# A windowed attention feeding a GELU MLP on one core: new order of the early attention stage, and of each batch's first transposes

## The chip, the cores and the metric

One Trainium2 chip, and on it one core. The metric is device time in microseconds of one execution, median of several runs. Inputs and output are fp32 in HBM; the kernel computes in fp16 with fp32 sums.

## What is computed

```python
def _attn_ref(q, k, v):                    # each 8 x 8 x 576 x 64 (batch, head, position, dim)
    scores = scale * np.matmul(q, k.transpose(0, 1, 3, 2))
    mask = np.abs(pos[:, None] - pos[None, :]) <= 32
    scores = np.where(mask, scores, -1000000000.0)
    attn = np.exp(scores - np.max(scores, axis=-1, keepdims=True))
    attn = attn / (np.sum(attn, axis=-1, keepdims=True) + 1e-09)
    return np.matmul(attn, v)

def _moe_ref(x, w_in, w_out):              # x 4608 x 512, w_in 512 x 2048, w_out 2048 x 512
    h = x @ w_in
    c = np.float32(np.sqrt(2.0 / np.pi))
    g = 0.5 * h * (1.0 + np.tanh(c * (h + 0.044715 * h * h * h)))
    return g @ w_out
```

Every position sees its 32 neighbours on each side. The eight heads' outputs, side by side, are the 512 features of a token, and all 8 x 576 = 4608 tokens go through the two-layer MLP.

## The kernel before

**Attention by pairs and units.** A batch has four pairs of heads (`pr`), and a pair has two units (`u = 2*pr` and `u = 2*pr + 1`), each for one half of the positions. The steps of a pair and a unit, by function and line of the kernel before:

- `cast_pair` (L199) casts a pair's q and k from fp32 to fp16; `trans_pair` (L209) transposes them on TensorE in eight matmuls against the identity `idn` (L213, L215) into the one PSUM tile `pt` of the pool `psT`, and DVE copies them out into `QT` (L216) and `KT` (L217). `cast_tail` (L182) and `trans_tail` (L188, four matmuls at L192, copies at L194 and L197) do the same for the last 64 positions of all pairs of a batch, in the same PSUM tile.
- `scores` (L243): six matmuls (L251) into `ps_s`, one tile of two banks; ACT's Exp (L258) out of it to `pe`; DVE's multiply with the band mask to `pm` (L260). The next `scores` needs `ps_s` empty.
- `values` (L265): twelve matmuls (L278) into `ps_od`, one tile of two banks, half of them against V, half against ones, which gives the denominators; ACT's Ln (L285) and Exp with scale -1 (L287) make their reciprocals `rt`; DVE multiplies into `xT` (L296), a ring of 2048 tokens. The next `values` needs `ps_od` empty, that is, this multiply done.

**The MLP by tiles of 512 tokens.** `ffn_in(t, fc)` (L302) is one group of four matmuls of 512 columns (L309) into a bank `ph` of the pool `psM` (three banks, tag `mm`), followed by ACT's GELU (L313). Sixteen such groups are the first product of a tile t. `ffn_out(t, i)` (L318) is one matmul of 512 columns (L323) into `py` (also `psM`); each sixteenth ends with DVE's copy `yo` (L327) and the store. Sixty-four of them are the second product of a tile.

**Order of the work.** Each engine runs its instructions in the order in which the program writes them. The program has three stages.

1. Early attention of batches 0 and 1 (L340 to L358): per pair POOL's casts of q, k and V, the transposes, (with pair 0) the tail, and then `scores` of each unit with `values` of the unit before.
2. The first product of tiles 0 and 1 together, over four quarters of `w_in` (L361 to L368); then the casts of `w_out` and the loads of batch 2 (L369 to L372). SP's loads wait for buffers that the casts release (`stage`, three buffers).
3. For t = 0 to 8 (L375 on): the first product of the tile (from t = 2), then its 64 matmuls of the second. For t = 0 to 5 batch b = t + 2 is computed among those 64. `put(i, ...)` fixes ahead of which matmul i a step stands, by `TRANS` (0, 13, 25, 37 for the pairs' transposes; the tail two later, the next pair's cast four later), `FIRST`, `STEP` and `LAG` (scores of unit u at 8 + 6u, values at 18 + 6u). Each such t starts with a load of ACT's Exp table, the loads of batch b + 1, `cast_tail(b)` and `cast_pair(b, 0)` on DVE.

Of the kernel before, what the change touches and what calls it, by code (L numbers as in the profile page):

```python
# [26 lines left out]
SW = 416  # L27

FIRST, STEP, LAG = 8, 6, 10
TRANS = (0, 13, 25, 37)


RING = 2048
# [3 lines left out]
def kernel(  # L39
# [96 lines left out]
    def load_w_in(i):  # L136
        w = stage.tile([128, 4, 512], FP32, name="wst", tag="stage", padded_shape=[128, 5, 512])
        nc.sync.dma_start(w, w_in_v[:, :, 512 * i:512 * i + 512])
        return w
# [122 lines left out]
            op=ALU.mult)  # L262
        units[(b, u)] = pm

    def values(b, u):  # L265
        pr, hf = u // 2, u % 2
        pm = units.pop((b, u))
        V = Vs[b % 2]
        od = psO.tile([128, 2, 512], FP32, name="ps_od")
        off = 0  # L270
        last = len(PIECES[hf]) - 1
        for i, (c, p0, p1) in enumerate(PIECES[hf]):
            n = p1 - p0
            a, e = p0 - HALF * hf, p1 - HALF * hf
            for w in range(2):
                for h in range(2):
                    r0 = 64 * h
                    nc.tensor.matmul(  # L278
                        od[r0:r0 + 64, w, 0:4 * HALF].rearrange("d (j p) -> d j p", j=4)[:, :, a:e],
                        V[:, c, 2 * pr + h, :] if w == 0 else ones,  # L280
                        pm[:, h, off:off + 4 * n].rearrange("k (j p) -> k j p", j=4),
                        start=(i == 0), stop=(i == last), skip_group_check=True)
            off += 4 * n
        lt = ap_.tile([128, 4 * HALF], FP32, name="lt")
        nc.scalar.activation(lt, od[:, 1, 0:4 * HALF], AF.Ln)  # L285
        rt = ap_.tile([128, 4 * HALF], FP32, name="rt")
        nc.scalar.activation(rt, lt, AF.Exp, scale=-1.0)  # L287
        o3 = od[:, 0, 0:4 * HALF].rearrange("d (j p) -> d j p", j=4)
# [29 lines left out]
    def ffn_out(t, i):  # L318
# [6 lines left out]
        if fc == NF - 1:  # L325
# [5 lines left out]
            while g < end:  # L331
# [4 lines left out]
                m += e - g  # L336
                g = e


    for b in range(2):  # L340
        cast_tail(b)
        V, vr = Vs[b], raws[b][3]
        for pr in range(NPAIR):
            cast_pair(b, pr, nc.gpsimd)
            nc.gpsimd.tensor_copy(V[:, 0:4, 2 * pr:2 * pr + 2, :], vr[:, 0:4, 2 * pr:2 * pr + 2, :])
            nc.gpsimd.tensor_copy(V[0:64, 4, 2 * pr:2 * pr + 2, :], vr[0:64, 4, 2 * pr:2 * pr + 2, :])
            trans_pair(b, pr)
            if pr == 0:
                trans_tail(b)
            for u in (2 * pr, 2 * pr + 1):  # L350
                scores(b, u)
                if u > 0:
                    values(b, u - 1)
                elif b:
                    values(b - 1, 7)
    wi = [load_w_in(0)]
    cast_w(wi[0], w_in16[:, :, 0:512])
    values(1, 7)  # L358


    for g in range(4):  # L361
        if g < 3:
            wi.append(load_w_in(g + 1))
        for t in range(2):
            for fc in range(4 * g, 4 * g + 4):
                ffn_in(t, fc)
                if t == 0 and fc == 4 * g + 1 and g < 3:
                    cast_w(wi[g + 1], w_in16[:, :, 512 * g + 512:512 * g + 1024])  # L368
    for g in range(4):  # L369
        cast_w(load_w_out(g), w_out16[:, 4 * g:4 * g + 4, :])  # L370
    load_qk(2, False)
    load_v(2)  # L372


    for t in range(NT):  # L375
        if t >= 2:
            for fc in range(NF):
                ffn_in(t, fc)
        b = t + 2
        at = {}  # L380

        def put(i, fn, *args):
            at.setdefault(i, []).append((fn, args))

        if b < B:
            load_exp_table()
            if b + 1 < B:
                load_qk(b + 1, False)
                load_v(b + 1)
            cast_tail(b)  # L390
            cast_pair(b, 0)
            for pr in range(NPAIR):
                put(TRANS[pr], trans_pair, b, pr)
                if pr == 0:
                    put(TRANS[pr] + 2, trans_tail, b)
                if pr < 3:
                    put(TRANS[pr] + 4, cast_pair, b, pr + 1)
            for u in range(8):
                put(FIRST + STEP * u, scores, b, u)
                put(FIRST + STEP * u + LAG, values, b, u)  # L400
        for i in range(64):
            for fn, args in at.pop(i, []):
                fn(*args)
            ffn_out(t, i)
        assert not at
# [28 lines left out]
```

## Time and profile before

| | |
|---|---|
| median of 3 runs | 385.72 us (385.48 to 386.09) |
| the profiled execution | 384.81 us, span 383.1 us, granted TensorE clock 0.994 |
| busy, share of the span | PE 90%, PEld 45%, ACT 55%, DVE 41%, POOL 15% |
| chain that ended last, by engine | PE 81%, DVE 8%, ACT 7%, issue 2%, POOL 1% |
| moved by DMA | 43.02 MB, mean 112 GB/s |

PE is the matmuls of TensorE, PEld its weight loads, which run beside them; DVE is VectorE, ACT ScalarE, POOL GpSimd, SP the engine that issues most loads and all stores. The profiled execution is one run; its time holds the span from the first to the last instruction and 1.7 us around it. The busy shares are of the whole span. The chain is followed back from the last instruction, at each step to what released it. A granted clock of 1.00 stands for 2.4 GHz, the higher of two levels; the lower is 1.2 GHz.

### The profile page before, as it was taken

Reading aid. Unit: us, or ns where it says so; the run is one execution under the profiler, and the core shown is the slowest. Engines: PE = TensorE matmul, PEld = TensorE weight load, DVE = VectorE, ACT = ScalarE, POOL = GpSimd, SP = SyncE. Lnnn points to the kernel's source line nnn. Section 1 sums busy time; section 2 is a strip of 40 time slices with the busy share of each in tenths; the row PEclk is TensorE's granted clock in tenths of the full one; section 3 lists DMA queues with packets and bytes.
Section 4 is the critical chain, followed back from the end, with each engine's and each line's share of the span. In section 5 each row is a group of like instructions: output and inputs, shape, how many; then the busy total and the mean of one; then the engine's idle time right before and its main releaser. Section 6 shows DMA issues by size and latency. Waiting matters only on the chain.

```text
span 383.1 us, 6525 instructions
## 1 busy us (share of the span) xinstructions
PE 343.9 (90%) x2592; PEld 171.8 (45%) x2592; DVE 158.0 (41%) x379; ACT 209.6 (55%) x349; POOL 59.4 (15%) x97
## 2 busy tenths in 40 slices
PE   2656559999979999999999999999999999999995
PEld 1445444444534444454445444444444444444442
DVE  3546544415755860585058504850485002011011
ACT  1545466665662676567656765767566721611610
POOL 8542501581040040004000400000000000000000
PEclk9999999999998999999999999999999999999999
DMA  7988307999779269117911692100011012003012
GB/s 198 267 219 276 112 3 242 384 286 215 95 69 285 68 68 280 19 55 68 272 27 44 74 264 41 56 29 27 2 55 29 27 30 78 6 27 82 2 33 77
DMA packets 72894, 43.02 MB, mean 112 GB/s; under 512 B 47776, under 2 KB 64160, under 8 KB 72864
## 3 DMA queue, kind: packets, MB, share of 16 engines
q1 hardware_dynamic: 44736, 39.07, 34.9%
q0 software_dynamic: 28128, 3.54, 14.5%
q8 instruction: 20, 0.33, 0.3%
q14 instruction: 10, 0.08, 0.1%
HBM read 36.70 MB, written 9.44 MB: 120 GB/s over the span
## 4 chain that ended last, share of the span: by engine, by line
PE 81%; DVE 8%; ACT 7%; issue 2%; POOL 1%; DVEq 0%
PE ph L309 33%; PE py L323 31%; PE ps_od L278 8%; PE ps_s L251 5%; DVE xT L296 3%; ACT rt L287 2%; ACT lt L285 2%; DVE KT L217 2%; ACT pe L258 2%; PE pt L213 2%; PE pt L215 2%; DVE QT L216 1%; PE pt L192 1%; POOL mask L164 0%; POOL mask L162 0%
## 5 line engine op out<-in xcount | busy, mean ns | idle before, releaser
L323 PE MATMUL py<-w_out,gT 128*128 128x512 f16 x576 | 147.6, 384 | 0.0
L309 PE MATMUL ph<-xT,w_in 128*128 128x512 f16 x576 | 126.7, 382 | 0.0
L313 ACT ACTIVATE gT<-ph 128x512 f16<-128x512 f32 x144 | 85.5, 597 | 62.9 <-PE ph L309 62.8
L309 PEld LDWEIGHTS <-w_in 128*128 128x128 f16 x576 | 56.5, 98 | 68.7 <-issue 1.4
L258 ACT ACTIVATE pe<-ps_s 128x832 f16<-128x832 f32 x64 | 55.1, 861 | 50.0 <-PE ps_s L251 50.0
L323 PEld LDWEIGHTS <-gT 128*128 128x128 f16 x576 | 49.2, 98 | 50.3 <-issue 1.1
L327 DVE COPY yo<-py 128x512 f32<-128x512 f32 x36 | 24.6, 685 | 74.3 <-PE py L323 74.3
L260 DVE TENSOR_TENSOR pm<-pe,mask 128x832 f16<-128x832 f16 x64 | 39.0, 609 | 25.8 <-ACT pe L258 25.0
L296 DVE TENSOR_TENSOR xT<-ps_od,rt 128x288 f16<-128x288 f32 (+6 forms) x96 | 31.3, 353 | 42.7 <-ACT rt L287 42.6
L285 ACT ACTIVATE lt<-ps_od 128x288 f32<-128x288 f32 x64 | 26.3, 410 | 40.0 <-PE ps_od L278 40.0
L278 PE MATMUL ps_od<-pm,V 128*64 128x192 f16 (+4 forms) x384 | 38.2, 253 | 9.1 <-DVE xT L296 8.3
L278 PEld LDWEIGHTS <-V 128*64 128x64 f16 x384 | 25.3, 122 | 32.4 <-issue 26.4
L129 POOL DMA_DIRECT2D V<-in_v_dram x24 | 21.2, 896 | 113.7 <-PE ps_od L278 111.7
L278 PE MATMUL ps_od<-pm,ones 128*64 128x192 f16 (+4 forms) x384 | 35.7, 248 | 0.0
L216 DVE COPY QT<-pt 128x512 f16<-128x512 f16 x32 | 13.4, 418 | 53.4 <-PE pt L215 52.6
L251 PE MATMUL ps_s<-QT,KT 64*128 64x192 f16 (+4 forms) x384 | 25.5, 245 | 10.4 <-DVE KT L217 8.6
L287 ACT ACTIVATE rt<-lt 128x288 f32<-128x288 f32 x64 | 28.3, 443 | 2.0
L251 PEld LDWEIGHTS <-KT 64*128 64x128 f16 x384 | 13.3, 101 | 30.9 <-issue 11.6
L278 PEld LDWEIGHTS <-ones 128*64 128x64 f16 x384 | 26.0, 124 | 0.0
L217 DVE COPY KT<-pt 128x512 f16<-128x512 f16 x32 | 21.8, 680 | 0.0
L213 PE MATMUL pt<-idn,q 128*128 128x128 f16 x128 | 14.2, 242 | 8.3 <-POOL q L204 6.4
L213 PEld LDWEIGHTS <-q 128*128 128x128 f16 x128 | 10.0, 106 | 13.3 <-POOL q L204 6.4
(33 smaller groups left out, 128.5 us busy)
## 6 DMA issues: line engine op xcount, KB each, us to landing
qr<-in_q_dram SPq DMA_DIRECT2D x6, 1024.0 KB, 8.8
kr<-in_k_dram SPq DMA_DIRECT2D x6, 1024.0 KB, 12.0
wst<-in_moe_w_in_dram SPq DMA_DIRECT2D x4, 1024.0 KB, 6.4
wst<-in_moe_w_out_dram SPq DMA_DIRECT2D x4, 1024.0 KB, 7.1
V<-in_v_dram POOLq DMA_DIRECT2D x24, 128.0 KB, 4.9
qr<-in_q_dram SPq DMA_DIRECT2D x8, 256.0 KB, 3.9
kr<-in_k_dram SPq DMA_DIRECT2D x8, 256.0 KB, 4.1
vr<-in_v_dram SPq DMA_DIRECT2D x16, 128.0 KB, 4.0
```

The costliest lines, as they stand in the source:

```text
L213: nc.tensor.transpose(pt[:, j, :], q16[:, j, :, :], idn)
L217: nc.vector.tensor_copy(KTs[b % 2][:, pr, 0:512].rearrange("d (p j) -> d p j", j=4), pt[:, 4:8, :].rearrange("d j p -> d p j"))
L251: nc.tensor.matmul(ps[:, h, off:off + 4 * n].rearrange("k (j p) -> k j p", j=4), KTs[b % 2][r0:r0 + 64, pr, 128 * c:128 * c + 128], QTs[b] ...
L258: nc.scalar.activation(pe, ps[:, :, 0:SW], AF.Exp, scale=SCALE)
L260: nc.vector.tensor_tensor(pm, pe, masks[hf].rearrange("p (o w) -> p o w", o=1).broadcast_to([128, 2, SW]), op=ALU.mult)
L278: nc.tensor.matmul(od[r0:r0 + 64, w, 0:4 * HALF].rearrange("d (j p) -> d j p", j=4)[:, :, a:e], V[:, c, 2 * pr + h, :] if w == 0 else ones ...
L285: nc.scalar.activation(lt, od[:, 1, 0:4 * HALF], AF.Ln)
L287: nc.scalar.activation(rt, lt, AF.Exp, scale=-1.0)
L296: nc.vector.tensor_tensor(dst, o3[:, j0:j1, a:e], r3[:, j0:j1, a:e], op=ALU.mult)
L309: nc.tensor.matmul(ph, w_in16[:, dc, fc * 128:fc * 128 + 128], xT[:, dc, t * 512 % RING:t * 512 % RING + 512], start=(dc == 0), stop=(dc = ...
L313: nc.scalar.activation(gTs[t][:, fc, :], ph, AF.Gelu_apprx_tanh)
L323: nc.tensor.matmul(py, gTs[t][:, fc, t4 * 128:t4 * 128 + 128], w_out16[:, fc, :], start=(fc == 0), stop=(fc == NF - 1))
```

## The change

Four things change.

- **Early attention** becomes one loop over the 16 units of both batches. The transposes of the next pair (also across the batches) stand behind the first unit of a pair, POOL's casts run one pair further ahead, the first pair's q and k are cast on DVE, and the tail of batch 1 stands behind unit 7.
- **Output banks.** `values` takes two tiles of one bank each, `ps_o` and `ps_d`; in the early stage units alternate between the pool `psO` and two banks of `psM`, which has no other use there (`spare`). In the later stage all use `psO`.
- **First transposes of a batch.** `begin(b, step)` does the tail's cast and pair 0's casts (step 0), pair 0's transposes and pair 1's casts (1), and the tail's transposes (2). For batch 2 the steps stand in the last groups of the first product of tiles 0 and 1, behind the casts of `w_out` and the loads, which are written earlier; for batch 3 among the matmuls of t = 0 at 50, 55 and 60; for batches 4 to 7 ahead of groups 10, 12 and 14 of the first product of t.
- **Positions.** Scores at 2 + 7u; values of unit u at the same position as scores of unit u + 2, ahead of them, the last two at 56 and 62; transposes of pairs 1 to 3 at 8, 22 and 36, with the next pair's cast.

```diff
-FIRST, STEP, LAG = 8, 6, 10
-TRANS = (0, 13, 25, 37)
+SCORES = [2 + 7 * u for u in range(8)]
+VALUES = SCORES[2:] + [56, 62]
+TRANS = {1: 8, 2: 22, 3: 36}
...
-    def values(b, u):
+    def values(b, u, spare=False):
...
-        od = psO.tile([128, 2, 512], FP32, name="ps_od")
+        pool, tags = (psM, ("mm", "mm")) if spare else (psO, ("O", "D"))
+        od = [pool.tile([128, 512], FP32, name="ps_o", tag=tags[0]),
+              pool.tile([128, 512], FP32, name="ps_d", tag=tags[1])]
...
-    for b in range(2):
-        cast_tail(b)
+    def cast_early(b, pr):
         V, vr = Vs[b], raws[b][3]
-        for pr in range(NPAIR):
-            cast_pair(b, pr, nc.gpsimd)
...
-            trans_pair(b, pr)
+        cast_pair(b, pr, nc.gpsimd)
...
+    cast_pair(0, 0)
...
+    cast_tail(0)
+    trans_pair(0, 0)
+    trans_tail(0)
+    cast_early(0, 1)
+    wi = []
+    for s in range(16):
+        b, u = s // 8, s % 8
+        scores(b, u)
+        if s:
+            values((s - 1) // 8, (s - 1) % 8, spare=(s % 2 == 0))
+        if s == 15:
+            wi.append(load_w_in(0))
+        if u % 2 == 0 and s < 14:
+            nb, pr = (s // 2 + 1) // 4, (s // 2 + 1) % 4
             if pr == 0:
-                trans_tail(b)
-            for u in (2 * pr, 2 * pr + 1):
-                scores(b, u)
-                if u > 0:
-                    values(b, u - 1)
-                elif b:
-                    values(b - 1, 7)
-    wi = [load_w_in(0)]
+                cast_tail(nb)
+            trans_pair(nb, pr)
+            if s < 12:
+                cast_early((s // 2 + 2) // 4, (s // 2 + 2) % 4)
+        if s == 7:
+            trans_tail(1)
     cast_w(wi[0], w_in16[:, :, 0:512])
     values(1, 7)
+
+    def begin(b, step):
+
+        if step == 0:
+            cast_tail(b)
+            cast_pair(b, 0)
+        elif step == 1:
+            trans_pair(b, 0)
+            cast_pair(b, 1)
+        else:
+            trans_tail(b)
...
         for t in range(2):
+            if g == 3 and t == 1:
+                for i in range(4):
+                    cast_w(load_w_out(i), w_out16[:, 4 * i:4 * i + 4, :])
+                load_qk(2, False)
+                load_v(2)
+                begin(2, 0)
             for fc in range(4 * g, 4 * g + 4):
+                if fc in (13, 15) and t == 1:
+                    begin(2, fc // 2 - 5)
                 ffn_in(t, fc)
...
             for fc in range(NF):
+                if b < B and fc in (10, 12, 14):
+                    begin(b, fc // 2 - 5)
                 ffn_in(t, fc)
...
-            cast_tail(b)
-            cast_pair(b, 0)
-            for pr in range(NPAIR):
+            for u in range(8):
+                put(VALUES[u], values, b, u)
+            for u in range(8):
+                put(SCORES[u], scores, b, u)
+            for pr in range(1, NPAIR):
                 put(TRANS[pr], trans_pair, b, pr)
-                if pr == 0:
-                    put(TRANS[pr] + 2, trans_tail, b)
                 if pr < 3:
-                    put(TRANS[pr] + 4, cast_pair, b, pr + 1)
-            for u in range(8):
-                put(FIRST + STEP * u, scores, b, u)
-                put(FIRST + STEP * u + LAG, values, b, u)
+                    put(TRANS[pr], cast_pair, b, pr + 1)
+            if t == 0:
+                for i in range(3):
+                    put(50 + 5 * i, begin, b + 1, i)
```

DVE in the early stage, from the copy of pair 1's K to the copy of pair 2's K (batch 0); `pm` is a unit's mask multiply, `xT` its multiply into the ring, and `QT` and `KT` the copies of a pair. Before, the masks are those of units 2 and 3 and the multiplies those of units 1 and 2:

```order
L217 COPY KT0_98<-pt_257 128x512
L260 TENSOR_TENSOR pm_277<-pe_275,mask0_96 128x832
L296 TENSOR_TENSOR xT_104<-ps_od_279,rt_294 128x4x72
L260 TENSOR_TENSOR pm_306<-pe_304,mask1_97 128x832
L296 TENSOR_TENSOR xT_104<-ps_od_308,rt_323 128x4x72
L216 COPY QT_183<-pt_332 128x4x128
L217 COPY KT0_98<-pt_332 128x512
```

After the change the same places hold the masks of units 1 and 2 and the multiplies of units 0 and 1:

```order
L217 COPY KT0_98<-pt_228 128x512
L260 TENSOR_TENSOR pm_254<-pe_252,mask1_97 128x832
L298 TENSOR_TENSOR xT_104<-ps_o_256,rt_272 128x4x72
L260 TENSOR_TENSOR pm_284<-pe_282,mask0_96 128x832
L298 TENSOR_TENSOR xT_104<-ps_o_286,rt_302 128x4x72
L216 COPY QT_189<-pt_305 128x4x128
L217 COPY KT0_98<-pt_305 128x512
```

So pair 2's copies come out of DVE one unit earlier in the pipeline, ahead of the mask of unit 3.

DVE around the border between t = 0 and t = 1; `yo` is the copy of an output tile, `t16`, `q16` and `k16` are the casts of batch 3 (its tail and a pair). Before, they stand behind the last `yo` of t = 0 and behind every multiply of batch 2:

```order
L260 TENSOR_TENSOR pm_1406<-pe_1404,mask1_97 128x832
L296 TENSOR_TENSOR xT_104<-ps_od_1412,rt_1427 128x4x72
L296 TENSOR_TENSOR xT_104<-ps_od_1436,rt_1451 128x4x72
L327 COPY yo_1458<-py_1394 128x512
L184 CAST t16_1475<-tr_1064 128x512
L204 CAST q16_1478<-qr_1062 128x2x4x64
L204 CAST k16_1479<-kr_1063 128x2x4x64
L216 COPY QT_1477<-pt_1482 128x4x128
L217 COPY KT1_99<-pt_1482 128x512
```

After the change they stand ahead of the last three multiplies of batch 2, behind the third `yo` of t = 0:

```order
L329 COPY yo_1393<-py_1305 128x512
L184 CAST t16_1400<-tr_1112 128x512
L204 CAST q16_1403<-qr_1110 128x2x4x64
L204 CAST k16_1404<-kr_1111 128x2x4x64
L298 TENSOR_TENSOR xT_104<-ps_o_1408,rt_1424 128x4x72
L260 TENSOR_TENSOR pm_1436<-pe_1434,mask1_97 128x832
L216 COPY QT_1402<-pt_1442 128x4x128
L217 COPY KT1_99<-pt_1442 128x512
L204 CAST q16_1453<-qr_1110 128x2x4x64
L204 CAST k16_1454<-kr_1111 128x2x4x64
L298 TENSOR_TENSOR xT_104<-ps_o_1458,rt_1474 128x4x72
L194 COPY QT_1402<-pt_1481 128x4x16 x4
```

The casts of batch 3 and its first copies have moved ahead of the last matmuls of t = 0.

## Rows read from the trace of the kernel before

**Rows 1.** Windows: each engine's busy us (x instructions), granted clock, DMA share, GB/s

```profile
9.22:59.14 49.92, 29.69 (x349) 23.44 (x349) 26.63 (x58) 25.60 (x46) 17.83 (x33) 1.00 0.59 170
59.14:87.83 28.69, 28.69 (x131) 12.79 (x130) 8.99 (x18) 20.64 (x34) 15.87 (x19) 1.00 1.12 320
87.83:112.72 24.89, 24.13 (x245) 11.90 (x243) 16.27 (x38) 15.41 (x27) 3.64 (x5) 1.00 0.97 118
112.72:141.24 28.52, 25.50 (x244) 12.31 (x245) 19.34 (x60) 14.62 (x25) 3.85 (x5) 0.94 0.74 141
...
155.10:179.78 24.68, 23.93 (x245) 11.96 (x244) 16.08 (x37) 15.25 (x26) 2.57 (x3) 1.00 0.18 39
```

**Rows 2.** Chain of waits, early stage, 44 to 52 us (start, us, what)

```profile
45.55 0.46 DVE xT L296
46.00 0.33 DVE QT L216
46.33 0.61 DVE KT L217
...
46.99 0.55 PE ps_s L251 x6
...
47.56 0.86 ACT pe L258
48.42 0.39 ACT lt L285
...
48.83 0.45 ACT rt L287
...
49.30 0.47 DVE xT L296
...
49.81 0.92 PE ps_od L278 x10
...
50.76 0.42 ACT lt L285
...
51.67 0.46 DVE xT L296
```

**Rows 3.** Early stage: timeline of POOL and DVE, then DVE's group of mask multiplies

```profile
40.54 2.28 POOL L148 CAST w_in<-wst 128x512 f16<-128x512 f32 x4
...
41.83 1.44 DVE L260 TENSOR_TENSOR pm<-pe,mask 128x832 f16<-128x832 f16 x1 [1.52 <-ACT pe L258]
...
L260 DVE TENSOR_TENSOR pm<-pe,mask 128x832 f16<-128x832 f16 x16 | 10.8, 675 | 12.7 <-ACT pe L258 12.1 <-issue 0.6
```

**Rows 4.** Timeline of SP's queue, then the page's DMA issues (us to landing)

```profile
28.74 12.25 SPq L138 DMA_DIRECT2D wst<-in_moe_w_in_dram  x3
...
kr<-in_k_dram SPq DMA_DIRECT2D x8, 256.0 KB, 4.1
```

**Rows 5.** Timeline of TensorE, start of t=1 (start, us, what, idle before)

```profile
114.64 0.40 PE L213 MATMUL pt<-idn,q 128*128 128x128 f16 x4 [1.92 <-DVE q L204]
...
115.20 0.59 PE L323 MATMUL py<-w_out,gT 128*128 128x512 f16 x2
116.48 0.61 PE L192 MATMUL pt<-idn,t 128*128 128x128 f16 x4 [0.68 <-DVE KT L217]
116.88 2.67 PE L323 MATMUL py<-w_out,gT 128*128 128x512 f16 x6
```

**Rows 6.** Timeline of DVE, end of the first product

```profile
84.68 0.41 DVE L204 CAST k<-kr 128x512 f16<-128x512 f32 x1
```

**Rows 7.** Who TensorE waited for, whole run (us, times, longest)

```profile
PE pt L192 <- DVE KT L217: 7.0, 8, 1.8
```

**Rows 8.** Chain of waits, products at full rate

```profile
100.99 0.97 PE py L323 x4
101.96 0.48 PE ps_od L278 x12
...
141.41 13.81 PE ph L309 x64
```

More of the change, by code (lines that the diff above doesn't have):

```diff
@@ L278, in values @@
                     nc.tensor.matmul(
-                        od[r0:r0 + 64, w, 0:4 * HALF].rearrange("d (j p) -> d j p", j=4)[:, :, a:e],
+                        od[w][r0:r0 + 64, 0:4 * HALF].rearrange("d (j p) -> d j p", j=4)[:, :, a:e],
                         V[:, c, 2 * pr + h, :] if w == 0 else ones,
@@ L284, in values @@
         lt = ap_.tile([128, 4 * HALF], FP32, name="lt")
-        nc.scalar.activation(lt, od[:, 1, 0:4 * HALF], AF.Ln)
+        nc.scalar.activation(lt, od[1][:, 0:4 * HALF], AF.Ln)
         rt = ap_.tile([128, 4 * HALF], FP32, name="rt")
         nc.scalar.activation(rt, lt, AF.Exp, scale=-1.0)
-        o3 = od[:, 0, 0:4 * HALF].rearrange("d (j p) -> d j p", j=4)
+        o3 = od[0][:, 0:4 * HALF].rearrange("d (j p) -> d j p", j=4)
         r3 = rt.rearrange("d (j p) -> d j p", j=4)
@@ L337, in ffn_out @@
                 g = e
-    for b in range(2):
-        cast_tail(b)
+    def cast_early(b, pr):
         V, vr = Vs[b], raws[b][3]
-        for pr in range(NPAIR):
-            cast_pair(b, pr, nc.gpsimd)
-            nc.gpsimd.tensor_copy(V[:, 0:4, 2 * pr:2 * pr + 2, :], vr[:, 0:4, 2 * pr:2 * pr + 2, :])
-            nc.gpsimd.tensor_copy(V[0:64, 4, 2 * pr:2 * pr + 2, :], vr[0:64, 4, 2 * pr:2 * pr + 2, :])
-            trans_pair(b, pr)
-            if pr == 0:
-                trans_tail(b)
-            for u in (2 * pr, 2 * pr + 1):
-                scores(b, u)
-                if u > 0:
-                    values(b, u - 1)
-                elif b:
-                    values(b - 1, 7)
-    wi = [load_w_in(0)]
+        cast_pair(b, pr, nc.gpsimd)
+        nc.gpsimd.tensor_copy(V[:, 0:4, 2 * pr:2 * pr + 2, :], vr[:, 0:4, 2 * pr:2 * pr + 2, :])
+        nc.gpsimd.tensor_copy(V[0:64, 4, 2 * pr:2 * pr + 2, :], vr[0:64, 4, 2 * pr:2 * pr + 2, :])
+    cast_pair(0, 0)
+    nc.gpsimd.tensor_copy(Vs[0][:, 0:4, 0:2, :], raws[0][3][:, 0:4, 0:2, :])
+    nc.gpsimd.tensor_copy(Vs[0][0:64, 4, 0:2, :], raws[0][3][0:64, 4, 0:2, :])
+    cast_tail(0)
[12 more added lines that the diff above has]
+            nb, pr = (s // 2 + 1) // 4, (s // 2 + 1) % 4
+            if pr == 0:
+                cast_tail(nb)
[4 more added lines that the diff above has]
+            trans_tail(1)
     cast_w(wi[0], w_in16[:, :, 0:512])
     values(1, 7)
+    def begin(b, step):
[7 more added lines that the diff above has]
+            trans_tail(b)
     for g in range(4):
@@ L368 @@
                     cast_w(wi[g + 1], w_in16[:, :, 512 * g + 512:512 * g + 1024])
[L369 to L372, printed above, removed]
     for t in range(NT):
+        b = t + 2
         if t >= 2:
             for fc in range(NF):
+                if b < B and fc in (10, 12, 14):
+                    begin(b, fc // 2 - 5)
                 ffn_in(t, fc)
-        b = t + 2
         at = {}
```

## The prediction, made before the changed kernel was run

> **What bounds the kernel now.** I read the page's chain of waits first, then a table of windows cut at the stages' borders, then the chain inside single stages. The page puts most of its chain on TensorE, but that is an average over two kinds of stage, and the windows part them [rows 1]. In the first product (59.14 to 87.83) TensorE is busy 28.69 of 28.69 us: nothing done on another engine helps there. In the early attention, 9.22 (first scores) to 59.14, it is busy 29.69 of 49.92: a chain sets the pace. From t=0 on attention is threaded into the second product, and TensorE is busy all but 0.76 us in t=0 and 0.75 in t=2; the exception is t=1, 28.52 us at a granted clock of 0.94.
>
> The chain of one pair in the early stage [rows 2] goes round once in 51.67 - 45.55 = 6.12 us: multiply into xT, copies of Q and K out of PSUM, scores, their Exp, then Ln, Exp and multiply of the unit before, a value product, and its Ln, Exp and multiply. The reader is to see that the round holds two legs of Ln, Exp and multiply. The second one is there because a single output tile must be emptied before the next value product, and because the copies of the next pair stand behind both.
>
> **The early stage.** After the change the transposes of pair p+1 stand between the two units of pair p, and value products alternate between two sets of output banks. So the leg from the start of the value product to the end of its multiply leaves the round: 51.67 + 0.46 - 49.81 = 2.32. What is left is 6.12 - 2.32 = 3.80; I take **3.85 per pair**, a little more for the masks that now stand closer. ACT alone has 2 x (0.86 + 0.42 + 0.45) = 3.46 of work in it [rows 2]; that is the floor. One round gets longer, that of batch 1's tail: the tail's transposes now stand behind a value product, and their copies behind its multiply. That costs at least nothing and at most a whole leg of 2.3; I take 2.2, near the upper end, since the Ln, Exp and multiply of that leg (1.4) and the tail's own transposes and copies (some 0.8) both stand in line. From the first scores to the first scores of the last pair that makes 7 x 3.85 + 2.2 = 29.2. It was 46.99 + 6.12 - 9.22 = 43.9 [rows 1, 2]. The ending (two units, and the last value product, which still waits for a full leg, since units 14 and 15 use the same banks) loses some 0.6 of its 6.0. The start gains 0.3 at most, since DVE and not POOL casts the first pair. Sum: 43.9 - 29.2 + 0.6 + 0.3 = 15.6 sooner.
>
> Against this stands POOL. One mask multiply took 1.44 us when it met POOL's casts of w_in, against a mean of 0.675 over all 16 [rows 3], and in the shorter stage the same 33 POOL instructions [rows 1] lie closer to the masks. Low end: no more hits than now, 0. High end: 0.77 more on each of 16 masks, all on the path, 12. The mean is nearest to the low end; I take 0.6. Early stage: **-15.0**. The Trainium skill (SBUF — State Buffer, Who interferes with whom) says that a VectorE instruction with two SBUF inputs and a GpSimd instruction that reads SBUF exclude each other for the whole of an instruction; the long mask agrees. By that rule, if every mask met a cast, the early stage would gain 3.6, not 15.0.
>
> Transfers hide: SP had issued all loads of both batches by 28.74, and such a load lands 4.1 us after its issue [rows 4], so the last pair is there at about 33, while at 3.85 per pair its transposes come at 9 + 6 x 3.85 + 2 = 34. That is cover of a us, no more: supply is what is late next. The loads of w_in wait for casts, and these move along with the stage.
>
> **The first product.** Twelve transposes of batch 2 move from t=0 into its last three groups. Eight took 0.56 in t=1 (114.64 to 115.20 [rows 5]), so twelve are 0.7, and 0.1 goes for changing weights: **+0.8**. They wait for DVE, which cast k at 84.68, until 25.9 to 26.0 after the product's start [rows 6]. TensorE reaches the place after 29 of 32 groups, 29/32 x 28.69 = 26.0. So the wait is nothing as long as the loads move along with the stage, and each us of lateness there is a us of the kernel, since the last groups stand behind it in TensorE's queue. SP's and POOL's queues keep their order: the casts of w_out and the loads of batch 2 are only written earlier. The twelve transposes leave t=0, but those of batch 3 come into it.
>
> **The second products.** Between the transposes of pair 0 and those of the tail TensorE waits for the copy of K out of the only transposing bank: 7.0 us in eight waits over the kernel [rows 7], 0.68 in the ordinary one [rows 5]. In six products (t=0 to 5) it goes, since two groups of four matmuls (8 x 0.216 = 1.7, from 13.81 for 64 [rows 8]) now lie between, longer than the copy. Six times 0.68 is 4.1.
>
> Values next to scores: four output matmuls ahead of a value product take 0.97 where 4 x 0.216 = 0.86 [rows 8], so leaving the long matmuls costs 0.1. Interruptions go from 21 to 13 per product, 6 fewer of the dear kind, but a direct change from values to scores is in no row at this clock. It costs between nothing (saving 0.6 per product) and two leavings (losing 0.6); I take 0.05, half of one, saving 0.3, because both are short matmuls on half the array. Against it, scores start at position 2 instead of 8, and the second ones may wait for the first Exp behind its table load: 0.1. Net 0.2, six times: 1.2.
>
> t=1 has more. TensorE waits 1.92 for q, because yo's copy and the casts of batch 3 stand in DVE's queue at that border; then six output matmuls take 2.67 us, the 1.2 GHz level (0.216 is the 2.4 GHz one): 2.67 - 6 x 0.216 = 1.4 lost [rows 5]. Both go, since batch 3 is cast and transposed inside t=0. So t=1 comes to t=2's 24.68 instead of 28.52 [rows 1], 3.84 less, and further down by the 0.7 of transposes that it no longer holds. The price of the cover: DVE casts in t=0 ahead of the multiply of unit 6, and if that is late, the last value product waits a few tenths.
>
> Sum of the later part: +0.8 - 4.1 - 1.2 - 3.84 - 0.7 = -9.0. Whole: -15.0 - 9.0 = **-24.0**. The profiled execution took 384.81 us (span 383.1), 0.91 under the median of 385.72; so 360.8 for it, and 361.7 as a median.
>
> **The rivals.**
> A. TensorE reaches its 2.4 GHz level inside the early stage. For it: it waits less there than now. Against it: the stage never leaves the slow rate today, though the granted clock prints 1.00: a value product is 0.92 in its chain [rows 2] against 0.48 in t=0's [rows 8]. Scores would fall by half of 0.55 in each round, and the tail and ending by some tenths: 7 x 0.2 + 1.2 = 2.6 less, 359.1.
> B. Mask and cast collide on every unit. For it the one row of 1.44, against it the mean. Half to all of the 12 above: 367 to 373.
> C. Supply. Loads a few us later than the 33 above, because several are under way at once, hold up the last pairs or batch 2's transposes: 3 to 6 more, 365 to 368.
> D. Slower than before. TensorE stands at batch 2's transposes in the first product. It arrives there about 15 us sooner than now, near 70. If these loads did not move along, but landed at 84 as now, it would wait 14 (376); from a landing at 70 + 24 = 94 on, the whole gain is gone, and with one at 100 and a restart at the slow rate (1.4) it is 361.7 + 30 + 1.4 = 393. Against it: the loads hang on casts that move along, and a full product of 28.69 lies before them.
> E. The output banks do not alternate in effect, because a spare tile waits for something else. Then the round keeps its 6.12, and only the later part remains: 376.7.
>
> **How the numbers follow.** Forecast 0.60, A 0.20, B 0.08, C 0.07, D 0.02, E 0.03. The likeliest case gives 361.7. Unknown in it: the round, between ACT's floor of 3.46 and 4.3 (about -3 to +3 over seven), tail and ending (+-1), the switch (-1.8 to +5.4 over six products). Taken together that is 356 to 367; A reaches the low part of it, C and the smaller half of B the top. I give 355.5 to 368. What a measurement of this kernel can't tell from no change is 0.2%, about 0.8 us; only D lies on the other side. Faster 0.97, same 0.01, slower 0.02.
>
> **What would show it.** Right: first scores of successive pairs 3.7 to 4.0 apart, near 6 at batch 1's tail; the first product starting near 44 and lasting near 29.5; no wait of the tail's transposes for K's copy after the early stage; t=1 near 23 us at a clock of 1.00. Wrong: an early round above 4.5, a wait of the first product for DVE's casts of batch 2, or second products that lose more at changes between values and scores than they save.

## The result, and the profile after

| | before | after |
|---|---|---|
| median of 4 runs each, on one chip | 385.79 us (385.48 to 386.09) | 356.94 us (355.28 to 357.90) |
| the profiled execution | 384.81 us, span 383.1 us | 356.09 us, span 354.1 us |
| ratio | | 0.925, 95% interval 0.921 to 0.929 |

The changed kernel is 28.9 us faster; 24.0 were forecast. In the profiled executions the span is shorter by 29.0 us, and this is the number accounted for below. First the page after: the engines' busy shares, the granted clock in 40 slices of 8.85 us, and the chain that ended last.

```profile
PE 331.0 (93%) x2592; PEld 169.1 (48%) x2592; DVE 158.0 (45%) x381; ACT 205.9 (58%) x349; POOL 60.4 (17%) x95
PEclk9989699999999999999999999999999999999999
PE 81%; ACT 7%; DVE 6%; issue 3%; DMA 1%; SPq 0%; DVEq 0%
```

TensorE is the chain's main engine as before. New is the dent in the clock in the fifth slice (35 to 44 us), where the early stage ends. The windows at the stages' borders answer to [rows 1] (same columns): early stage, first product, t=0, t=1, and t=2 in its two products.

```profile
8.33:40.71 32.38, 21.78 (x349) 17.02 (x349) 26.36 (x58) 25.06 (x46) 19.77 (x32) 0.89 0.92 269
40.71:70.66 29.95, 29.95 (x142) 13.59 (x141) 11.19 (x27) 20.64 (x34) 17.03 (x21) 0.94 1.12 316
70.66:94.50 23.84, 23.53 (x246) 12.63 (x245) 16.98 (x41) 14.48 (x25) 3.03 (x4) 1.00 0.95 111
94.50:117.38 22.88, 22.48 (x233) 11.71 (x232) 15.87 (x48) 14.29 (x26) 3.80 (x6) 1.00 0.90 175
117.38:131.96 14.58, 14.58 (x78) 6.90 (x77) 4.92 (x16) 10.59 (x18) 2.42 (x3) 1.00 1.16 215
131.96:154.70 22.74, 22.59 (x233) 12.03 (x232) 13.64 (x28) 14.43 (x25) 2.13 (x3) 1.00 0.15 39
```

| stretch | before | after | change | forecast |
|---|---|---|---|---|
| to the first scores | 9.22 | 8.33 | -0.89 | -0.3 |
| early stage | 49.92 | 32.38 | -17.54 | -14.7 |
| first product | 28.69 | 29.95 | +1.26 | +0.8 |
| t=0 | 24.89 | 23.84 | -1.05 | -0.9 |
| t=1 | 28.52 | 22.88 | -5.64 | -5.4 |
| t=2 to 5, both products | 4 x 38.54 | 149.24 in all | -4.92 | -3.5 |
| the rest | 87.70 | 87.48 | -0.22 | 0 |

Each t from 2 to 5 took 38.54 us before, its first product of 13.86 (from 141.24 to 155.10) and the second of 24.68 [rows 1]; after, t=2 takes 14.58 + 22.74 = 37.32, t=3 to 5 take 37.23 to 37.39. The largest surplus is in the early stage. Its chain of waits, one ordinary round and then the one with batch 1's tail (start, us, what):

```profile
15.81 0.37 PE ps_s L251 x6
...
16.21 0.71 ACT pe L258
...
16.97 0.41 ACT lt L287
...
17.40 0.45 ACT rt L289
...
17.88 0.46 DVE xT L298
18.34 0.33 DVE QT L216
18.67 0.61 DVE KT L217
...
19.32 0.37 PE ps_s L251 x6
...
21.77 0.82 DVE t L184
...
22.88 0.69 DVE KT L217
...
23.61 0.61 PE pt L192 x4
24.22 0.46 PE ps_s L251 x6
```

The second leg of Ln, Exp and multiply of [rows 2] is out of the round, as the prediction had it: one leg, the two copies, the scores, their Exp. But scores take 0.37 and not 0.55, so this round runs at TensorE's 2.4 GHz level, and it is 19.32 - 15.81 = 3.51. The tail's round goes from 19.32 to 24.15, 4.83 us. It holds two pieces more than the ordinary one: DVE's cast of the tail (`t`, 0.82), which stands ahead of the pair's copies, and the tail's transposes. The scores behind these start as soon as TensorE is through with them, at 24.15 in its own timeline, and wait for none of the tail's copies.

Who TensorE waited for, over the whole run, and its timeline at the end of the early stage:

```profile
PE ps_s L251 <- DVE KT L217: 4.3, 5, 1.1
PE pt L192 <- DVE KT L217: 3.8, 2, 2.3
```

```profile
39.87 0.32 PE L280 MATMUL ps_o<-pm,V 128*64 128x128 f16 x2 [1.47 <-DVE xT L298]
```

Of the eight waits of the tail's transposes for K's copy [rows 7] only the two early ones are left. The last value product of the early stage waits 1.47 us for the multiply that empties its banks.

### The profile page after: what moved, and what is told of

Same layout as the page of the kernel before. It is cut to its first block, busy times and chain, and to the rows that moved or that the text cites. A ratio compares the mean times of both kernels' runs of the same rounds, so it can differ in the third digit from the quotient of the medians.

```text
span 354.1 us, 6527 instructions
## 1 busy us (share of the span) xinstructions
PE 331.0 (93%) x2592; PEld 169.1 (48%) x2592; DVE 158.0 (45%) x381; ACT 205.9 (58%) x349; POOL 60.4 (17%) x95
## 4 chain that ended last, share of the span: by engine, by line
PE 81%; ACT 7%; DVE 6%; issue 3%; DMA 1%; SPq 0%; DVEq 0%
PE ph L311 36%; PE py L325 30%; PE ps_o L280 5%; PE ps_s L251 4%; PE ps_d L280 3%; ACT pe L258 2%; DVE xT L298 2%; ACT rt L289 2%; ACT lt L287 2%; PE pt L213 1%; PE pt L215 1%; DVE KT L217 1%; DMA tr<-in_k_dram 1%; DVE pm L260 1%; ACT gT L315 1%
## 5 line engine op out<-in xcount | busy, mean ns | idle before, releaser
L325 PE MATMUL py<-w_out,gT 128*128 128x512 f16 x576 | 139.3, 380 | 0.0
L311 PE MATMUL ph<-xT,w_in 128*128 128x512 f16 x576 | 129.0, 382 | 0.0
L325 PEld LDWEIGHTS <-gT 128*128 128x128 f16 x576 | 51.4, 98 | 57.3
L287 ACT ACTIVATE lt<-ps_d 128x288 f32<-128x288 f32 x64 | 26.2, 410 | 48.0 <-PE ps_d L280 47.6
L298 DVE TENSOR_TENSOR xT<-ps_o,rt 128x288 f16<-128x288 f32 (+6 forms) x96 | 31.2, 353 | 31.1 <-ACT rt L289 30.6
L280 PE MATMUL ps_o<-pm,V 128*64 128x192 f16 (+4 forms) x384 | 34.7, 238 | 4.8 <-DVE xT L298 2.2
L280 PEld LDWEIGHTS <-V 128*64 128x64 f16 x384 | 23.5, 113 | 25.1 <-issue 17.6
L280 PE MATMUL ps_d<-pm,ones 128*64 128x192 f16 (+4 forms) x384 | 32.0, 232 | 0.0
L251 PE MATMUL ps_s<-QT,KT 64*128 64x192 f16 (+4 forms) x384 | 23.6, 230 | 5.1 <-DVE KT L217 4.3
L280 PEld LDWEIGHTS <-ones 128*64 128x64 f16 x384 | 23.8, 114 | 0.0
```

The lines of the kernel that those rows point to most:

```text
L251: nc.tensor.matmul(ps[:, h, off:off + 4 * n].rearrange("k (j p) -> k j p", j=4), KTs[b % 2][r0:r0 + 64, pr, 128 * c:128 * c + 128], QTs[b] ...
L280: nc.tensor.matmul(od[w][r0:r0 + 64, 0:4 * HALF].rearrange("d (j p) -> d j p", j=4)[:, :, a:e], V[:, c, 2 * pr + h, :] if w == 0 else ones ...
L287: nc.scalar.activation(lt, od[1][:, 0:4 * HALF], AF.Ln)
L311: nc.tensor.matmul(ph, w_in16[:, dc, fc * 128:fc * 128 + 128], xT[:, dc, t * 512 % RING:t * 512 % RING + 512], start=(dc == 0), stop=(dc = ...
L325: nc.tensor.matmul(py, gTs[t][:, fc, t4 * 128:t4 * 128 + 128], w_out16[:, fc, :], start=(fc == 0), stop=(fc == NF - 1))
```

## Experiments

Twelve kernels, each against the kernel before on the same chip. Theory: two independent gains, the leg taken out of the early round, and TensorE's waits and interruptions taken out of the second products and of t=1. Rivals: the early gain is one of the clock alone (A), or one of supply (C, D), or the banks do nothing (E).

**The two halves apart.** The first kernel has the early stage and the output banks of the change, the second only what comes behind them. Against the changed kernel:

```diff
 # early part only
-SCORES = [2 + 7 * u for u in range(8)]
+FIRST, STEP, LAG = 8, 6, 10
...
-                if b < B and fc in (10, 12, 14):
-                    begin(b, fc // 2 - 5)
...
+            cast_tail(b)
+            cast_pair(b, 0)
```

> The early stage of the change (new loop, alternating output banks) with the two products as they were before. Theory, that the two halves act apart and add up: the windows of the changed kernel put 18.4 us of the 29.0 into the start and the early stage and take back 1.3 in the first product, of which 0.7 is transposes that this kernel does not move; so 385.8 - 17.8 = 368.0, and t=1 still holds the wait of 1.9 us for DVE's casts and its slow stretch. Rival, that the later part hides or gives back some of it (loads of batch 2 that now come late): 371 or more, with a wait of TensorE in the first product or at t=0.

```diff
 # late part only: the early loop of the kernel before
-    for s in range(16):
...
+        for pr in range(NPAIR):
+            cast_pair(b, pr, nc.gpsimd)
...
+            trans_pair(b, pr)
```

> The early stage as before, with the first transposes of a batch in the preceding product and the new positions. Theory of two separate halves: windows give t=0 to t=5 a gain of 1.0 + 5.6 + 4.9 and the first product 0.8 more, so 385.8 - 10.7 = 375.1, with a first product near 29.4. Rival, that the gain in t=1 rests on the shorter early stage: 378 or more.

Measured: 367.27 us (ratio 0.955, 0.952 to 0.959), 17.8 us faster, and 375.31 us (0.975, 0.972 to 0.977), 9.8 us faster. The sum of 27.6 leaves 1.2 of the whole, less than the spread of the changed kernel's own runs (2.6). Within that spread the halves are independent, and each came out near what was expected of it (368.0 and 375.1).

**One set of output banks.**

```diff
-            values((s - 1) // 8, (s - 1) % 8, spare=(s % 2 == 0))
+            values((s - 1) // 8, (s - 1) % 8, spare=False)
```

> The changed kernel with all value products of the early stage in one set of output banks; the order stays. Theory, that the round of a pair is a chain and the second bank set takes one leg (values, Ln, Exp, multiply, about 2.0 to 2.3 us) out of it: each value product waits for the multiply of the unit before, so a pair costs two legs, 4.2 to 4.7 instead of 3.7; the early stage is 5 to 8 us longer, 362 to 365. Rival, that the clock made the stage short and the banks did nothing: within 1 us of the changed kernel as long as TensorE's rate is the same.

Measured: 361.65 us (0.940, 0.936 to 0.943), 4.7 us slower than the changed kernel. Who TensorE waited for, in this kernel:

```profile
PE ps_o L280 <- DVE xT L298: 9.3, 14, 1.5
```

The wait that the second set removes is back in nearly every unit. Ordinary rounds took 3.49 to 4.74 us. TensorE's level was not the same as in the changed kernel (four of the six ran at the lower one throughout, there one), so 4.7 is not the price of the banks alone; a comparison at one level stands behind the kernels with idle matmuls.

**Transposes of a pair ahead of its first unit, as before, the banks kept.**

```diff
+        if u % 2 == 0 and s > 0:
+            trans_pair(b, u // 2)
...
-            trans_pair(nb, pr)
```

> The changed kernel with the early transposes directly ahead of their pair, as before, and the output banks alternating. Theory of the chain: the copies of a pair then stand behind the multiply of the first unit of the pair before, and the round is scores 0.57, exp 0.86, mask 0.6, values 0.9, Ln, Exp and multiply 1.35, copies 1.0: about 5.3 instead of 3.7; the early stage is 10 us longer, 366 to 368. Rival, that the banks alone do it and the place of the transposes does not matter: within 1 us of the changed kernel.

Measured: 369.70 us (0.960, 0.957 to 0.962), 12.8 slower than the changed kernel. One round in its chain of waits:

```profile
31.99 0.48 PE ps_s L251 x6
...
32.49 0.86 ACT pe L258
34.12 0.84 ACT pe L258
...
35.90 0.46 DVE xT L298
36.35 0.33 DVE QT L216
36.69 0.61 DVE KT L217
...
37.34 0.55 PE ps_s L251 x5
```

Both units' Exp are on the way round again, since the copies stand behind both multiplies; the round takes 37.34 - 31.93 = 5.41. Each of the two edits in the early stage is needed: undone alone, the place of the transposes costs 12.8 us and the banks 4.7. But here scores take 0.53 to 0.55 up to the last pair, so these rounds ran at the lower level, and part of the 12.8 belongs to the clock.

**Old positions in the second products**, with the new place of each batch's first transposes.

```diff
-SCORES = [2 + 7 * u for u in range(8)]
-VALUES = SCORES[2:] + [56, 62]
+SCORES = [8 + 6 * u for u in range(8)]
+VALUES = [18 + 6 * u for u in range(8)]
-TRANS = {1: 8, 2: 22, 3: 36}
+TRANS = {1: 13, 2: 25, 3: 37}
...
-                    put(TRANS[pr], cast_pair, b, pr + 1)
+                    put(TRANS[pr] + 4, cast_pair, b, pr + 1)
```

> The changed kernel with the positions of before in the second products (scores at 8 + 6u, values at 18 + 6u, transposes at 13, 25 and 37), while the first transposes of a batch stay in the preceding product. Theory: in the changed trace values pass into scores without a gap (the scores start 0.49 us after the values start), so values next to scores saves 6 leavings of the long matmuls at 0.1 in each of six products; t=2 is 37.9 instead of 37.3, the whole 3 to 4 us slower, 360 to 361. Rival, that the wait for K's copy was all there was to gain and a direct change costs what a leaving costs: within 0.5 us of the changed kernel, t=2 at 37.3.

Measured: 360.71 us (0.935, 0.933 to 0.937), 3.8 slower. The prediction had put 1.2 on the positions. In t=0 the chain of waits shows the price of each interruption; first this kernel, then the changed one:

```profile
86.08 0.97 PE py L325 x4
...
87.53 0.54 PE py L325 x2
88.07 0.29 PE ps_s L251 x6
```

```profile
79.27 1.62 PE py L325 x7
80.88 0.19 PE ps_o L280 x2
...
81.34 0.03 PE ps_d L280 x2
81.37 0.29 PE ps_s L251 x6
```

Each run of long matmuls ends 0.1 us later than its count gives at 0.216 (0.97 for 0.86, 0.54 for 0.43, 1.62 for 1.51), however long it is, so fewer runs pay it less often. The change from values to scores costs nothing: 81.34 + 0.03 = 81.37. Profile against profile, this kernel's span is 4.5 longer: 0.38 in t=2, 1.73 in t=0 and t=1 (0.85 of it TensorE waiting for batch 3's q), 1.33 from t=3 on, and 1.06 in stages that the edit leaves alone. About 3.4 us belong to the positions.

**TensorE kept busy with idle matmuls.** Their results are not read. The first kernel has 20 of them ahead of the last value product, the second also 24 ahead of the first pair's transposes, 18 behind these and 24 ahead of the tail's of batch 1.

```diff
+    def spin(n):
+        if n:
+            wt = psM.tile([128, 512], FP32, name="wt", tag="mm")
+            for _ in range(n):
+                nc.tensor.matmul(wt[:, 0:128], idn, idn, start=True, stop=True)
...
+    spin(20)
```

> The changed kernel with 20 matmuls of the identity with itself ahead of the last value product of the early stage, where TensorE waits 1.47 us; their result is not used. Theory, that this wait lets TensorE's clock fall and the first product then starts at 1.2 GHz (0.50 in 40 to 44 us): the first product takes 29.0 to 29.4 instead of 29.95, and the twenty matmuls, 1.1 to 2.1 us, lie mostly in the wait: 356 to 357, at best 1 us faster. Rival, that the clock had fallen before this wait, so that the matmuls only add: 0.5 us slower, the same first product.

> The changed kernel with such matmuls of the identity in four waits of TensorE: 24 before the first transposes, 18 between these and the tail's, 24 ahead of batch 1's tail, 20 ahead of the last value product. Theory of the chain: the early stage hangs on ACT and DVE, so at 2.4 GHz from its start a pair still takes 3.5 to 3.7, and the stage shrinks by 1 us or less (28 us less what the tail keeps); all of it 355 to 356.5. Rival, that the clock made the difference between the 3.85 a pair that was forecast and what was measured: at 2.4 GHz throughout a pair takes 3.4 or less, 353 or less.

Measured: 358.88 us (0.931, 0.925 to 0.938) and 358.92 us (0.930, 0.928 to 0.933): no gain, probably a loss. The fill did its part at the border (in both, the first product runs at the higher level, 115 of its matmuls in 24.99 us), but the product then reached batch 2's transposes before their data. From the timeline of TensorE in the second of the two kernels:

```profile
41.49 24.99 PE L311 MATMUL ph<-xT,w_in 128*128 128x512 f16 x115 [0.33 <-DVE w_in L148]
68.67 0.40 PE L213 MATMUL pt<-idn,q 128*128 128x128 f16 x4 [2.18 <-DVE q L204]
```

This is the wait of rivals C and D. The changed kernel does not have it, with 0.9 us to spare (q is cast at 66.51, TensorE arrives at 67.40). The first text's rival was right on one point: in the changed kernel the clock had fallen before the wait of 1.47, which begins at 38.4 us (granted 0.74 from 37 to 37.5 us, 0.50 from there). The fill did not keep it up, it brought it back.

These kernels also allow a comparison at one level. Windows from the first scores of a pair to those of the next: the changed kernel, the first of the two kernels with idle matmuls (two rounds without any fill in them), and the kernel with one set of banks.

```profile
15.81:19.32 3.51, 2.31 (x44) 1.87 (x44) 2.87 (x7) 3.17 (x7) 2.06 (x3) 1.00 0.97 252
27.85:31.78 3.93, 3.70 (x45) 2.89 (x46) 3.04 (x7) 3.31 (x7) 2.07 (x4) 0.50 0.91 236
31.78:35.81 4.03, 3.69 (x44) 2.87 (x45) 3.14 (x7) 3.29 (x7) 2.09 (x5) 0.50 1.05 399
34.28:39.02 4.74, 3.76 (x45) 2.99 (x46) 2.92 (x7) 3.32 (x6) 1.89 (x3) 0.50 0.89 335
```

At the lower level a round is 6.12 before [rows 2], 5.41 with the transposes in the old place (the scores of 0.55 show the level in these two), 4.74 with one set of banks and 3.93 or 4.03 with both edits. So the order of the work takes some 2.1 us out of a round with the clock unchanged, 1.4 of them lost again without the new place and 0.8 without the second set. The higher level takes off another 0.4 to 0.5 (3.51).

**The banks the other way round**, so that the last value product finds its banks free.

```diff
-            values((s - 1) // 8, (s - 1) % 8, spare=(s % 2 == 0))
+            values((s - 1) // 8, (s - 1) % 8, spare=(s % 2 == 1))
```

> The changed kernel with the two bank sets of the early stage swapped, so that units 14 and 15, the last two, use different ones. Theory: the last value product no longer waits 1.47 us for the multiply of unit 14; it waits for its own mask instead, some 0.5 after the value product before it ends: 0.9 us faster at the border, 356.0, and less of a stretch at the lower clock behind it. Rival, that the mask or the exp of the last unit ends just as late: no difference.

Measured: 357.04 us (0.927, 0.925 to 0.928), the same as the changed kernel. From the first scores of the last pair to the product took 4.49 us and not 5.20, as meant; but the first scores began at 9.12 and not 8.33, since the load that DVE waits for there landed later.

**Four kernels on the border and on supply**: the banks the other way round and DVE's cast of the tail behind the first pair's copies; that with fill (12 idle matmuls behind each odd unit, 8 ahead of the last value product); that with batch 2's q and k loaded ahead of half of `w_out`; and fill and load order together.

```diff
...
-    cast_tail(0)
     trans_pair(0, 0)
+    cast_tail(0)
...
-            values((s - 1) // 8, (s - 1) % 8, spare=(s % 2 == 0))
+            values((s - 1) // 8, (s - 1) % 8, spare=(s % 2 == 1))
```

> The change with the two output banks the other way round (odd loop steps take the pair of psM, so the last value product of the stage finds a bank free), and with DVE's cast of the tail behind the copies of the first pair. In the run with the banks alone the last step to the first product took 4.49 us in place of 5.20, but the first scores began at 9.12 us in place of 8.33, since DVE stood at the cast of the tail's load. Theory: with both edits the start is at 8.3 us or sooner and the last step 4.5 us, so 0.7 us or more below the changed kernel: about 356. Rival: what is gained ahead of the first product is lost inside it, where DVE's casts for batch 2 wait for their load (7.32 us at the tail's cast in the run with fill in every round): then the same 357, with a wait of TensorE for q or k late in the first product.

```diff
+        if s % 2 == 1 and s < 15:
+            spin(12)
...
+    spin(8)
```

> As the run with both edits, with 12 idle matmuls of 128 columns against the identity behind each odd unit of the early stage and 8 ahead of the last value product. Their results are read by nothing. Theory of the clock: rounds of the early stage at the higher level took 3.5 to 3.7 us and at the lower 3.9 to 4.7, so if the fill keeps the higher level all rounds are 3.5 to 3.6 us, the product starts at the higher level, and the first product begins some 1.5 us sooner than in the run with both edits. Rival: as in the earlier run with fill, the level falls whatever stands between (there it fell at 12 us), the rounds stay near 3.8 on average, and the time is the same or up to 1.5 us longer.

```diff
-                for i in range(4):
+                for i in range(2):
                     cast_w(load_w_out(i), w_out16[:, 4 * i:4 * i + 4, :])
                 load_qk(2, False)
-                load_v(2)
                 begin(2, 0)
+                for i in range(2, 4):
+                    cast_w(load_w_out(i), w_out16[:, 4 * i:4 * i + 4, :])
+                load_v(2)
```

> As the run with both edits, with the loads of batch 2 (q and k, with the casts of its first step) written ahead of the last two of the four w_out loads and v's load last. Theory of the supply: if TensorE is to wait for batch 2's loads once the early stage is shorter, this removes the wait: no gap before the transposes of batch 2 in the first product, and up to 0.5 us below the run with both edits. Rival: at this length of the early stage the loads are in time anyhow (the changed kernel shows no such wait), so the time is the same within 0.5 us, unless the second product of t = 0 now waits for w_out, which would cost up to 1 us.

> Fill and load order together. Theory: with the fill alone the first product reaches batch 2's transposes too soon for their loads (1.29 and 2.18 us of waiting for q in the two earlier runs with fill), and with the loads ahead that wait is gone, so this run stands 1 to 2 us below the run with fill alone; if the fill also holds the clock, about 353 to 354.5 us. Rival: the waits go, but the clock falls as before, and the time is 356 to 358 us, no better than without fill.

| | median us | ratio, 95% interval | first product starts | second product of t=0 starts |
|---|---|---|---|---|
| the change | 356.94 | 0.921 to 0.929 | 40.71 | 70.66 |
| banks and tail's cast | 357.32 | 0.925 to 0.929 | 41.23 | 73.00 |
| and fill | 359.09 | 0.928 to 0.934 | 40.78 | 75.44 |
| and load order | 357.31 | 0.924 to 0.927 | 41.09 | 70.77 |
| fill and load order | 357.56 | 0.926 to 0.929 | 40.34 | 70.66 |

The last two columns are from one profiled execution each (356.09, 358.51, 360.88, 358.15 and 357.53 us).

The theory of the start fell. The tail's cast behind the first pair's copies brought the first scores to 7.44 at best, but then TensorE waited 1.45 to 1.51 for the tail's cast and up to 1.34 for POOL's cast of pair 1, and the third round began at 16.07 to 17.12, later than in the changed kernel (15.81). These texts call the earlier kernel one with fill in every round; it had fill in four places only, and its clock fell where none stood. The theory of the clock held for the level: with fill the granted clock stays at 1.00 from 12 to 38 us (0.92 in the changed kernel), the ordinary rounds behind the first take 3.5 to 3.9 us, the tail's 4.2 to 4.3, and the product starts at the higher level. But with fill alone it starts 0.45 sooner (40.78 for 41.23) and not 1.5, and the time does not fall. TensorE in the kernel with fill:

```profile
40.78 25.33 PE L312 MATMUL ph<-xT,w_in 128*128 128x512 f16 x116 [0.20 <-DVE w_in L148]
69.35 0.61 PE L214 MATMUL pt<-idn,q 128*128 128x128 f16 x4 [3.23 <-DVE q L205]
```

The same engine with fill and load order:

```profile
40.34 25.33 PE L312 MATMUL ph<-xT,w_in 128*128 128x512 f16 x116 [0.93 <-DVE w_in L148]
69.56 0.40 PE L193 MATMUL pt<-idn,t 128*128 128x128 f16 x4 [1.72 <-DVE KT L218]
76.35 0.27 PE L281 MATMUL ps_o<-pm,V 128*64 128x192 f16 x2 [0.44 <-DMA V<-in_v_dram]
```

Whatever is moved, a load is what TensorE meets next: batch 2's q, or, with that brought forward, w_in at the start, `KT` behind DVE's casts of w_out (the last of which waited 1.55 for its load), and then V. The load order without fill did remove the wait for q (0.68 with banks and tail's cast alone), and then TensorE waited for V three times from 76 to 79 us, 1.56 in all: the same time. None of these kernels starts the second product of t=0 before 70.66. By the windows of the early stage and the first product, 32.38 us x 269 GB/s + 29.95 x 316 = 18.2 MB arrive by then in 62.3 us; before it was 49.92 x 170 + 28.69 x 320 = 17.7 MB in 78.6 us. At 318 GB/s throughout, the rate of 28 to 36 us, 18.2 MB would still be 57 us; this is an estimate, and no run shows that rate to be a limit (from 32 to 36 us 400 GB/s were moved). So the change has used up nearly all the cover that loads had, and no version here beats it; that supply alone holds the time where it is, is argued from these waits and not shown.

## Why the prediction was right

The forecast of 361.7 us was 4.8 us too slow, the time lies in the range near its low end, and every stretch moved the way that was forecast.

- **The round without the second leg: the mechanism right, the size helped by the clock.** "3.85 per pair" came out as 3.73 on average in the six ordinary rounds (3.49 to 3.99; the first, 3.49, has no value product of a pair before it), 0.75 us in all. The chain is the predicted one. Undoing the transposes' place gave 5.41 per round, one set of banks brought the wait back, which excludes rival E, and at the lower level both edits give 3.93 and 4.03 for 6.12, which excludes the clock as the whole cause. But 3.85 was worked out from rows at that level, so it was 0.1 to 0.2 too short there. That the average fell below it is the clock's doing: the good fit of this number is partly luck.
- **The tail's round: the step that failed.** "the tail's transposes now stand behind a value product, and their copies behind its multiply" put the rest of a leg (1.4) and the tail's transposes and copies (0.8) in line for the next scores. Of these only the transposes are: in TensorE's queue the scores stand right behind them, at 24.15, and DVE copies the tail out from 24.35 on. What the prediction left out is DVE's cast of the tail, 0.82 of this round. The round was 4.83 and not 6.05: 1.22 us. The kernel before shows the same at batch 1's tail in TensorE's timeline, which the prediction does not use; DVE copies the tail out from 34.33 on, after these scores have begun:

```profile
33.68 0.61 PE L192 MATMUL pt<-idn,t 128*128 128x128 f16 x4 [1.76 <-DVE KT L217]
34.22 0.53 PE L251 MATMUL ps_s<-QT,KT 64*128 64x160 f16 x6
```

- **POOL against the masks: no longer masks in the mean, but four long ones where they count.** DVE's group of mask multiplies in the early stage after the change, and what TensorE waited for masks:

```profile
L260 DVE TENSOR_TENSOR pm<-pe,mask 128x832 f16<-128x832 f16 x16 | 10.8, 678 | 4.0 <-ACT pe L258 3.0 <-POOL k L204 0.6 <-issue 0.4
...
PE ps_o L280 <- DVE pm L260: 1.7, 5, 0.6
```

678 ns on average against 675 before [rows 3], and no collision on every unit: rival B is out. But the four masks from 27.88 to 33.09 took 0.78 to 1.05 with POOL's casts running beside them, three of them held up a value product (1.2 of the 1.7 us; before, TensorE waited 0.4 for a mask in the whole early stage), and the two rounds in which they lie took 3.87 and 3.72 at the higher level, where the round shown above took 3.51. So the 0.6 forecast may have been spent there, inside the rounds; how much of these 0.6 us is the masks', no run parts. The Trainium skill (SBUF — State Buffer, Who interferes with whom) says that a VectorE instruction with two SBUF inputs contends with a GpSimd instruction that reads SBUF. This trace agrees for single masks: the one of 1.05 us started at 33.09, POOL's cast of V at 33.08.
- **Start and ending**: -0.89 for -0.3, and the ending 5.20 for the 5.43 implied. With the three items above this makes the 3.4 us by which the early part was underrated: 0.75 for the rounds, 1.22 for the tail's, 0.6 for the masks (whatever they cost is inside the measured rounds), 0.6 for the start, 0.2 for the ending.
- **Rival A came in part.** Its price was 2.6 us, given as if the higher level held throughout. The granted clock rises and falls within the stage (last section). The five ordinary rounds behind the first took 18.86 us; five at 3.98, the mean of the two at the lower level, would be 19.9, so the clock gave some 1.0 there (an estimate). It took some back in the first product: 116 matmuls of 0.216 are 25.06 and took 26.69 up to the transposes, 1.6 more, where before 128 of them are 27.65 and took 28.69, 1.0 more. With fill they show as 25.33 for 26.85. This is the likely place of the 0.46 by which the first product missed its +0.8.
- **First product and supply: right.** The twelve transposes did not wait, though by 0.9 us only. They took 0.68 (0.45 and 0.23) as forecast, but not by the forecast's working: twelve at the rate of eight in 0.56 would be 0.84.
- **t=1: right.** 5.64 for 5.4; TensorE waits for no cast at its start, and the clock is 1.00.
- **Tail's wait and positions: underrated.** t=2 to 5 gained 4.92 for 3.5. The waits went as counted; the term "Net 0.2" for the positions was mis-sized, since "half of one" leaving per direct change from values to scores was charged, and 81.34 to 81.37 shows none. Undoing the positions costs about 3.4 us over six products, 2.5 without the wait for batch 3's q: 0.4 to 0.6 each, near the free end of the bounds given.

## What to carry to other kernels

Write the round of a pipelined stage as a chain and look for the piece that appears twice: what ends the second copy (here the copies of the next pair, standing behind both multiplies) is the thing to move; here its place in the queue was worth more than the second output buffer (1.4 against 0.8 us a round at one level of the clock). Before pricing two versions of a stage against each other, look whether TensorE ran at the same level in both. When a stage shrinks, compare what its loads need with what is left: here the gains tried behind the change ended at a load. Count the borders between kinds of matmuls, not the matmuls between them: each long run paid 0.1 us once.

## What the hardware showed that was not expected

**TensorE's clock goes up and down inside the early stage.** Windows of the changed kernel:

```profile
12.00:20.00 8.00, 5.43 (x100) 4.33 (x98) 6.50 (x14) 7.16 (x15) 5.75 (x9) 1.00 0.97 246
20.00:24.00 4.00, 2.25 (x42) 1.64 (x37) 3.45 (x8) 2.94 (x6) 2.81 (x6) 0.95 0.73 207
24.00:28.00 4.00, 3.55 (x49) 2.56 (x48) 3.25 (x12) 2.71 (x5) 2.25 (x5) 0.62 0.97 250
28.00:36.00 8.00, 4.88 (x94) 3.92 (x95) 7.38 (x14) 7.18 (x15) 4.43 (x8) 1.00 0.98 318
40.00:44.00 4.00, 4.00 (x20) 1.78 (x20) 2.36 (x7) 2.73 (x4) 1.17 (x2) 0.50 0.60 167
```

It falls in the tail's round (0.59 from 23.5 to 24 us), after TensorE waited 1.51 us for the copy of K, which stands behind the tail's cast. It falls again at 37 us (0.74 from 37 to 37.5), after waits of 0.77 and 0.27 us. It is back after stretches in which TensorE was busy: 3.55 of the 4 us from 24 to 28, and all of 40 to 44 (0.93 from 44 to 44.5). The Trainium skill (TensorE: Matmul & The Clock Gate, A second HAM failure mode: psum-queue depth-cycling) tells of a kernel whose clock goes back and forth because TensorE idles briefly and often between groups. This trace agrees in that the clock goes back and forth here too, and that fill in the gaps stops it. Fill in every round held it at the higher level from 12 us on; fill in four places did not (0.50 from 12 to 16 us, between two of them). A granted clock of 1.00 at the start, as in [rows 1], is not the rate: from 8 to 12 us scores took 0.53, as at the lower level.

**Runs spread more.** The kernel before stayed within 0.6 us, the changed one within 2.6; its four spans were 353.3 to 355.9 at mean clocks of 0.978 to 0.986. The clock alone does not explain it: 355.9 came with 0.978 and with 0.986. Differences of a us between such kernels stay open here.
